# Small products of the last head on four column groups: head 31's last values, its selection, a sum of squares and three sums

## The chip, the cores and the metric

The kernel runs on one NeuronCore of one Trainium2 chip. Its time is the device time of one execution in microseconds; lower is better. TensorE (PE) multiplies, VectorE (DVE), ScalarE (ACT) and GpSimd (POOL) work on vectors, and SyncE (SP) issues nearly all DMAs.

## The reference

One decode step of a transformer block for 4 batches with one token each, all in fp32: an adaptive layer norm, attention with 32 query heads on 8 key and value heads over 4096 cached positions, a gated residual, a second adaptive layer norm, and a token-mixing MLP with F = 1792.

```python
mod = (silu(c) @ w_mod).reshape(4, 6, 1, 512)
sa, ca, ga, sb, cb, gb = (mod[:, k] for k in range(6))
h = layernorm(x) * (1 + ca) + sa
q = (h @ wq) heads;  p = softmax(q k^T / sqrt(128));  o = p v      # k, v: (4, 8, 4096, 128)
x = x + ga * (o @ wo)
h = layernorm(x) * (1 + cb) + sb
u = gelu(layernorm(h)[.., None] * w1 + b1)                          # (4, 512, 1792)
x = x + gb * (u @ w2 + b2)
```

Keys and values are 4 x 8 x 4096 x 128 x 4 bytes each, 134 MB together; they are read once.

## The kernel before, in words

The 32 pairs of batch and key head are called heads 0 to 31 here. SP loads their keys and values in order into a ring of three slots. For each head PE makes the scores, DVE their maximum, ACT the exponentials, DVE turns them (`turn`), PE multiplies them by the values (`values`, `values_narrow`), DVE copies the result out of PSUM (`copy_v`), PE picks and turns the four query rows out of it with the matrix `eight` (`pick`), DVE scales them (`copy_o`), and PE multiplies by the output weights (`project`).

From head 23 on the order of all steps is written out by hand in the string `PLAN`, where `v31.1` is a part of head 31's value products, `V31` the copy, `z31` the turned values, `a31` pick, `A31` copy_o, `I` the addition of the residual `ep`, `p31` project. Each engine runs its own instructions in that order; a wait holds up all that is behind it on that engine.

Head 31's values come as the last data of the cache, in five pieces (blocks of 128 positions 0 to 15, 16 to 23, 24 to 27, 28 to 29, 30 to 31). `values_narrow` multiplies block j with 32 columns of weights (the probabilities) and 128 columns of data (the values), on column group j mod 4 of the array. Blocks 30 and 31 go another way (`values_turned`): the values are the weights, all 128 columns of them, and the four probabilities the moving data, added straight into the PSUM tile `pt` that `pick` then adds the selection to.

Behind `p31` (PSUM tile `pgx`) lies a chain that everything after it needs: DVE makes `a` from `pgx` (`centre`, L617), ACT squares (L622), DVE makes two products (L626, L627), PE spreads `a` to all partitions (`spread_last`, tile `ph`, in two halves), sums the squares over partitions (`deviation`, tile `psq`, L636) and sums three columns (`moments`, tile `pmo`, L641), ACT takes a root (`sd`), DVE forms `vr` (L642, L646, L648) and `hb` (L656), POOL a power (L100), DVE `br` (L658), and then ACT and DVE apply the gelu to 14 pieces of the last batch (L551, L556, L428) while PE contracts them (`py3`, L433).

An fp32 product is two passes on PE: order counts products, the trace counts a weight load (PEld) and a matmul (PE) for each pass. PSUM tiles come from pools: `ps_m` has two slots for tiles tagged `m`, `ps_v` has one slot, tagged `pv`; a tile that takes over a slot waits for the earlier tile's users.

Of the kernel before, what the change touches and what calls it, by code (L numbers as in the profile page):

```python
# [8 lines left out]
F32 = mybir.dt.float32  # L9
# [6 lines left out]
REP = HQ // HKV  # L16
NF = F // 128
EPS = 1e-5
P = 128
NS = B * HKV  # L20
# [8 lines left out]
def adaln_decode(ctx: ExitStack, tc: tile.TileContext, small, x, wmod, wq, kk, kv, vv, wo, out):  # L29
# [8 lines left out]
    ps_v = ctx.enter_context(tc.tile_pool(name="ps_v", bufs=1, space=PSUM))  # L38
    ps_m = ctx.enter_context(tc.tile_pool(name="ps_m", bufs=2, space=PSUM))
    ps_e = ctx.enter_context(tc.tile_pool(name="ps_e", bufs=1, space=PSUM))  # L40
    ctx.enter_context(tc.manual_schedule())
    mm = nc.tensor.matmul
# [41 lines left out]
    mine = g32[:, 8 * (B - 1):8 * (B - 1) + 1]  # L84
    mid = cst.tile([P, 1], F32, name="mid")
    nc.gpsimd.tensor_scalar(mid, mine, 1.0 / D, None, op0=OP.mult)
    eight = g32.rearrange("p (r x) -> p r x", x=8)[:, :, 0]
# [69 lines left out]
    KT, VT, WM = {}, {}, {}  # L157

    def slots():
        return ring.tile([P, 2, SK], F32, name="kv", tag="kv")  # L160
# [35 lines left out]
    def load_key(t, i):  # L196
        nc.sync.dma_start(t, kv[i - 2][:, 0])
        key(t, i)

    def load_v(t, i, cuts):  # L200
        value(t, i)
        src = (kv[i][:, 1] if i < NS - 2 else vv[i - NS + 2]).rearrange("p (j d) -> p j d", d=DH)
        for lo, hi in zip(cuts, cuts[1:]):
            nc.sync.dma_start(VT[i][:, lo:hi], src[:, lo:hi])
# [58 lines left out]
    def turn(i, halves=None):  # L263

        S.pop(i, None)
        if halves is None:
            dv.transpose(PL[i][0], PL[i][0])  # L267
            return
        for n in halves:
            p = PL[i][0][:, n * 512:(n + 1) * 512]  # L270
            dv.transpose(p, p)
# [22 lines left out]
    def values_narrow(i, ks, pv=None):  # L294
        if ks[0] == 0:
            PV[i] = ps_v.tile([P, DH], F32, name="pvn", tag="pv") if pv is None else pv
        pv = PV[i]
        pT = PL[i][0].rearrange("p (k r) -> p k r", r=32)
        top = 32 if i < NS - 1 else 30
        for k in ks:  # L300
            for j in range(4 * k, min(4 * k + 4, top)):
                c = j % 4
                mm(pv[32 * c:32 * c + 32, :], pT[:, j, :], VT[i][:, j, :], start=(k == 0), stop=(j + 4 >= top))  # L303

    def values_turned(i):
        pT = PL[i][0].rearrange("p (k r) -> p k r", r=32)
        OT[i] = pt = ps_m.tile([P, REP], F32, name="pt", tag="m")
        for j in (30, 31):
            mm(pt, VT[i][:, j, :], pT[:, j, 0:32:8], start=(j == 30), stop=False)

    def copy_v(i):
        pv = PV[i]
# [3 lines left out]
    ACC, OT = {}, {}  # L316

    def pick(i):
        po = PV.pop(i)
        n, m = po.shape[-1] // DH, WIDE.get(i, 1)  # L320
        if i in OT:
            mm(OT[i], po, eight, start=False, stop=True)
            return
        pt = ps_m.tile([P, m, REP], F32, name="pt", tag="m")
        OT[i] = pt[:, 0]
        for c in range(n):
            sel = sel4[:, c, :] if n > 1 else eight
            mm(pt, po[:, c * DH:(c + 1) * DH], sel.unsqueeze(1).to_broadcast([P, m, REP]),  # L328
               start=(c == 0), stop=(c == n - 1))
# [7 lines left out]
    def project(i, pa=None, between=None):  # L337
        b, h = divmod(i, HKV)
        oT = OT[i]
        if pa is None:  # L340
            pa = ps_m.tile([P, D], F32, name="pa", tag="m")
            for g in range(REP):
                mm(pa[32 * g:32 * g + 32, :], oT[:, g:g + 1].to_broadcast([P, 32]), wo_t[h][:, g, :],  # L343
                   start=True, stop=True)
        else:
            for g in range(REP):
                for c in range(4):
                    mm(pa[32 * c:32 * c + 32, :], oT[:, g:g + 1].to_broadcast([P, 32]),  # L348
                       wo_t[h][:, g, c * P:(c + 1) * P], start=(g == 0 and h == HKV - 2),
                       stop=(g == REP - 1 and h == HKV - 1))  # L350
                if between and g == 1:
                    between()
        PA[i] = pa
# [242 lines left out]
    mom = cst.tile([P, 3], F32, name="mom")  # L596
    sq = cst.tile([P, 1], F32, name="sq")
# [35 lines left out]

    def deviation():
        ps = ps_m.tile([P, 1], F32, name="psq", tag="m")
        mm(ps, mine.to_broadcast([P, P]), sq, start=True, stop=True)  # L636
        nc.scalar.activation(sd, ps, AF.Sqrt, bias=epsc, scale=1.0 / D)

    def moments():
        pg = ps_m.tile([P, 3], F32, name="pmo", tag="m")  # L640
        mm(pg, mid.to_broadcast([P, P]), mom, start=True, stop=True)  # L641
        dv.tensor_scalar(vr[:, 0:1], pg[:, 0:1], pg[:, 0:1], pg[:, 1:2], op0=OP.mult, op1=OP.subtract)  # L642
        return pg

# [35 lines left out]
    for i in range(NS - HKV):  # L680
# [30 lines left out]
        if i == 2:  # L711
            for t in range(2, 5):
                pm = mod(t)
                dst = prep[:, {2: 1, 3: 2, 4: 3}[t]]
# [12 lines left out]
    pve = pgx = pc = ep = spare = slot = None  # L727
    gates = list(range(2 * REP))
    cuts = {NS - 1: (0, 16, 24, 28, 30, 32), NS - 2: (0, 16, 32)}
    last, halves = [(0, 1, 2, 3), (4, 5), (6,), (7,)], [(0, 1), (2, 3), (4, 5), (6, 7)]  # L730
    PLAN = """
    a23 v24.0 A23 p23 t25.0 P23 F R v24.1 LP25 G s26 t25.1 M H V24 LP26 Q a24 S26 v25.0 N s27 x A24 f p24 g
    x LP27 m26 S27 P24 m27 X26 X27 b26 B26 e26 x b27 v25.1 c g t26.1 l25 t26.0 B27 s28 V25 c g L25
# [1 line left out]
    LK30 t27.1 S29 P26 v27.0 m29 l27 g LK31 T t28.1 X29 LT t28.0 s30 L27 S30 b29 v27.1 B29 e29 l28 m30 V27  # L735
    LV28 L28 a27 g X30 t29.1 t29.0 l29 L29 s31 A27 LV29 b30 p27 x B30 S31 c c m31 e30 P27 X31 v28.0 f LT LV30
    b31 v28.1 B31 f e31 LV31 l30 V28 L30 t30.1 l31 L31 a28 t31.1 A28 p28 v29.0 v29.1 t30.0 f P28 V29 v30.0 a29
    v30.1 A29 LW p29 f v30.2 v30.3 t31.0 P29 g V30 Y y a30 A30 p30 E x v31.0 f v31.1 v31.2 v31.3 V31 z31 a31 I A31 j zy p31
    g T2 za zs zr zc0 zp0 zq zg zp1 zm zc1 T3 zn zw0
    """  # L740
    TABLE = {"s": scores, "S": row_max, "m": turn_max, "X": col_max, "b": spread_max, "B": copy_max, "e": expo,
# [4 lines left out]
    for step in PLAN.split():  # L746
        op, k = step.rstrip("0123456789."), step.lstrip("abcdefghijklmnopqrstuvwxyzABCDEFGHIJKLMNOPQRSTUVWXYZ")
        i, q = (int(n) for n in (k + ".0").split(".")[:2]) if k else (0, 0)
        if op in TABLE:
            TABLE[op](i)  # L750
        elif op in MIX:
            MIX[op]()
        elif op == "t":
            turn(i, [q])
        elif op == "v":
            if i < NS - 2:
                (values if i < NARROW else values_narrow)(i, range(4 * q, 4 * q + 4))
                continue
            if i == NS - 2 and q == 0:
                pve = ps_s.tile([P, 8, P], F32, name="pve", tag="s")  # L760
            values_narrow(i, (last if i == NS - 1 else halves)[q], pve[:, 4 * (NS - 1 - i)])
        elif step == "z31":
            values_turned(i)
        elif op == "p":
            project(i, pgx[:, 4] if i >= NS - 2 else None, mean_last if i == NS - 1 else None)
        elif op == "LT":
            slot = slots()
        elif op == "LK":
            load_key(slot[:, i % 2], i)
        elif op == "LV":  # L770
            load_v(slot[:, i % 2], i, cuts.get(i, (0, 32)))
        elif op == "LW":
            spare = load_wm5()
        elif op == "x":
            mix.expand(spare if mix.n == 6 else None)
        elif op == "f":
            fold_gate(gate, gates[:1])
            del gates[:1]
        elif step == "T":
            nc.scalar.activation(tab, neg1, AF.Exp)  # L780
        elif op == "Y":
            pgx = ps_s.tile([P, 8, P], F32, name="pgx", tag="s")
        elif op == "y":
            pc = fold_groups(ps_m, ACC.pop(B - 1), "m")
        elif op == "E":
            ep = cst.tile([P, P], F32, name="ep")
            dv.tensor_mul(ep, pc, prep[:, 1])
            dv.tensor_tensor_reduce(ep, ep, prep[:, 0], g32[:, 8 * (B - 1):8 * (B - 1) + 1], 0.0, OP.add, OP.add,
                                    tally[:, 0:1])
        elif op == "I":  # L790
            mm(pgx[:, 4], ident, ep, start=False, stop=False)
        elif step == "T2":
            nc.scalar.activation(tab, ones[0:1, 0:1], AF.Sqrt)
        elif step == "T3":
            nc.scalar.activation(tab, neg1, AF.Gelu_apprx_tanh)
        elif op == "za":
            al = centre(pgx[:, 4])
        elif op == "zs":
            squares(pgx[:, 4])
        elif op == "zr":  # L800
            products(al)
        elif op == "zp":
            if i == 0:
                ph = ps_s.tile([P, D], F32, name="ph3", tag="s")
            spread_last(ph, al, range(2 * i, 2 * i + 2))
        elif op == "zc":
            mix.fold_rest(i)
        elif op == "zg":
            pg = moments()
        elif op == "zm":  # L810
            variance(pg)
        elif op == "zn":
            hb, wr, br = affine_last(ph)
        elif op == "j":
            tally_up()
        elif op == "zw":
            modmm(pgx[:, 0], 5, (0,))
# [36 lines left out]
```

## Time and profile before

| what | value |
|---|---|
| time, median of 3 runs | 385.89 us (385.88 to 386.0) |
| the profiled execution, time and span | 385.9 us, 384.1 us |
| PE, PEld busy | 290.1 us (2412 matmuls), 117.2 us (2412 loads) |
| DVE, ACT, POOL busy | 199.4, 111.9, 9.0 us |
| HBM read | 157.32 MB, 410 GB/s over the span |
| granted TensorE clock | mean 0.916; full from about 241 us to the end |

The span is the time from the first to the last instruction of the profiled execution; 1.8 us of its own time lie around it. In rows of the timeline the first number is the start in us from the span's start, the second the time from the first start to the last end of the group, and `x` a count; `128*32` is rows and columns of the array that the instruction uses, and what follows a bracket's arrow is what ended the idle time before the group. In rows of the chain of waits the second number is the time that the chain spends there.

### The profile page before, as it was taken

How to read it: one execution, taken by the hardware profiler on the slowest of the kernel's cores; microseconds unless marked ns; L12 is line 12 of the kernel's file. 1: busy time of each engine (PE TensorE's matmuls, PEld its weight loads, DVE VectorE, ACT ScalarE, POOL GpSimd, SP SyncE). 2: the span in 40 equal slices, each digit the busy share in tenths (PEclk: the TensorE clock that was granted, in tenths of full speed). 3: DMA queues.
4: the chain of work that ended last, by engine and by line, in shares of the span. 5: the costliest groups of instructions: out<-in, count | busy, mean ns of one | idle time of the engine just before them, and what ended most of it. 6: DMA issues, size and time to landing. Idle time of an engine off the chain costs nothing.

```text
span 384.1 us, 5670 instructions
## 1 busy us (share of the span) xinstructions
PE 290.1 (76%) x2412; PEld 117.2 (31%) x2412; DVE 199.4 (52%) x414; ACT 111.9 (29%) x143; POOL 9.0 (2%) x34
## 2 busy tenths in 40 slices
PE   0958484973855928798777879988887887889984
PEld 0112121320222302234222223342222344333673
DVE  0130531440442714556666544657665567778777
ACT  1001210121110111113457310214675104757266
POOL 2100000000000000000000000000000000000000
PEclk9979956697896979989999995999999999999999
DMA  8999999999999999999999999999999999999930
GB/s 332 437 437 437 403 459 427 411 440 433 421 439 437 435 437 433 432 433 432 427 428 433 433 427 432 433 435 437 437 428 430 432 432 431 416 431 426 417 142 4
DMA packets 7410, 157.70 MB, mean 411 GB/s; under 512 B 964, under 2 KB 1236, under 8 KB 1496
## 3 DMA queue, kind: packets, MB, share of 16 engines
q1 hardware_dynamic: 7376, 157.33, 95.5%
q8 instruction: 19, 0.31, 0.3%
q14 instruction: 7, 0.06, 0.0%
q10 hardware_dynamic: 8, 0.00, 0.0%
HBM read 157.32 MB, written 0.01 MB: 410 GB/s over the span
## 4 chain that ended last, share of the span: by engine, by line
DMA 60%; PE 29%; DVE 8%; ACT 2%; issue 1%; POOL 0%; SPq 0%; DVEq 0%; ACTq 0%
DMA kv<-in_kv 58%; PE s L231 7%; PE pv L291 7%; PE s L122 3%; PE qs L138 2%; DVE p L267 2%; DVE m L236 2%; DMA sm<-in_small 2%; PE pa L343 2%; PE pt L328 2%; ACT wo L556 1%; PE pb L251 1%; PE pve L303 1%; PE pm L240 1%; PE pgx L348 1%
## 5 line engine op out<-in xcount | busy, mean ns | idle before, releaser
L231 PE MATMUL s<-kv,QT 128*32 128x512 f32 x512 | 71.8, 685 | 48.7 <-DMA kv<-in_kv 48.4
L236 DVE TENSOR_REDUCE m<-s 128x1 f32<-128x1024 f32 x32 | 39.2, 1224 | 100.7 <-PE s L231 100.7
L261 ACT ACTIVATE p<-s,nm 128x1024 f32<-128x1024 f32 x32 | 35.6, 1114 | 181.2 <-DVE nm L256 181.1
L291 PE MATMUL pv<-kv,p 128*32 128x512 f32 x464 | 67.8, 652 | 0.6 <-DMA kv<-in_kv 0.6
L231 PEld LDWEIGHTS s<-kv,QT 128*32 128x32 f32 x512 | 15.3, 119 | 91.0 <-DMA kv<-in_kv 62.9
L328 PEld LDWEIGHTS pt<-g,po 128*128 128x128 f32 x236 | 30.6, 202 | 27.6 <-issue 20.3
L343 PE MATMUL pa<-wo,oT 128*32 128x512 f32 x240 | 33.7, 633 | 4.9 <-DVE oT L335 4.7
L328 PE MATMUL pt<-g,po 128*128 128x4 f32 (+2 forms) x236 | 33.4, 265 | 1.5 <-DVE po L314 1.0
L267 DVE STREAM_TRANSPOSE p<-p 128x1024 f32<-128x1024 f32 x25 | 30.9, 1235 | 0.0
L314 DVE COPY po<-pv 128x512 f32<-128x512 f32 x29 | 20.0, 689 | 15.7 <-PE pv L291 15.6
L245 DVE TENSOR_REDUCE mx<-pm 1x128 f32<-1x512 f32 x32 | 21.3, 669 | 0.9 <-PE pm L240 0.9
L428 DVE TENSOR_SCALAR u<-hb,wr,sm 128x512 f32<-128x512 f32 x40 | 19.9, 540 | 1.9 <-POOL wr L423 1.0
L485 ACT ACTIVATE u<-u 128x1024 f32<-128x1024 f32 x20 | 20.4, 1052 | 1.5 <-DVE u L428 1.4
L261 ACT ACT_TABLE_LOAD x11 | 14.1, 1283 | 21.9 <-DVE nm L256 21.8
L361 DVE TENSOR_TENSOR acc<-acc,pa 128x512 f32<-128x512 f32 x26 | 17.8, 686 | 2.2 <-PE pa L343 2.1
L251 PEld LDWEIGHTS pb<-neg,mx 1*128 1x128 f32 x64 | 10.0, 194 | 27.6 <-DVE mx L245 25.9
L122 PE MATMUL s<-wm,sT 128*4 128x512 f32 x16 | 9.9, 788 | 10.4 <-POOL sT L108 10.4
L485 ACT ACT_TABLE_LOAD x13 | 16.7, 1283 | 0.2
L291 PEld LDWEIGHTS pv<-kv,p 128*32 128x32 f32 x464 | 13.6, 146 | 6.8 <-issue 2.8
L240 PE MATMUL pm<-ident,m 128*1 128x128 f32 x32 | 8.9, 280 | 7.6 <-DVE m L236 3.5
L251 PE MATMUL pb<-neg,mx 1*128 1x1 f32 x64 | 12.7, 265 | 2.1 <-DVE mx L245 2.1
L240 PEld LDWEIGHTS pm<-ident,m 128*1 128x1 f32 x32 | 2.5, 80 | 34.6 <-DVE rl L280 25.6
(173 smaller groups left out, 227.6 us busy)
## 6 DMA issues: line engine op xcount, KB each, us to landing
kv<-in_kv SPq DMA_DIRECT2D x28, 4096.0 KB, 22.0
wq<-in_wq SPq DMA_DIRECT2D x2, 4096.0 KB, 16.1
wo<-in_wo SPq DMA_DIRECT2D x4, 2048.0 KB
kv<-in_kv SPq DMA_DIRECT2D x4, 2048.0 KB, 21.1
wm<-in_wmod SPq DMA_DIRECT2D x2, 2048.0 KB, 16.1
kv<-in_kk SPq DMA_DIRECT2D x1, 4096.0 KB
kv<-in_vv SPq DMA_DIRECT2D x3, 1024.0 KB
wm<-in_wmod SPq DMA_DIRECT2D x1, 1024.0 KB
```

Of the source, the lines that this page charges most:

```text
L122: mm(s0[0:B, t * D:(t + 1) * D], sT[:, k, :], wm01[:, t, k, :], start=(k == 0), stop=(k == 3))
L231: mm(s[32 * c:32 * c + 32, n * 512:(n + 1) * 512], QT[:, b, h, :], KT[i][:, (n * 4 + c) * 512:(n * 4 + c + 1) * 512], start=True, stop=True)
L236: dv.tensor_reduce(M[i], S[i], axis=AX.X, op=OP.max)
L245: dv.tensor_reduce(mx, M[i].rearrange("o (c r) -> o r c", c=4).unsqueeze(1).to_broadcast([1, 4, 32, 4]), axis=AX.X, op=OP.max)
L251: mm(pb, M[i].rearrange("o c r -> o (c r)"), neg1, start=True, stop=True)
L261: nc.scalar.activation(p, S[i], AF.Exp, bias=M.pop(i), accum_out=l)
L267: dv.transpose(PL[i][0], PL[i][0])
L291: mm(PV[i][32 * q:32 * q + 32, :], pT[:, 128 * k:128 * k + 128:4], VT[i][:, 4 * k:4 * k + 4, :].rearrange("p j d -> p (j d)"), start=(k < ...
L314: dv.tensor_copy(PV[i], pv)
L328: mm(pt, po[:, c * DH:(c + 1) * DH], sel.unsqueeze(1).to_broadcast([P, m, REP]), start=(c == 0), stop=(c == n - 1))
L343: mm(pa[32 * g:32 * g + 32, :], oT[:, g:g + 1].to_broadcast([P, 32]), wo_t[h][:, g, :], start=True, stop=True)
L485: nc.scalar.activation(u, u, AF.Gelu_apprx_tanh)
```

## The change

Four things become four products each, of 32 weight columns, one on each column group of the array, by a new helper `quarters`: the turned values, the selection of head 31, the sum of squares and the three sums. Of head 31's values, blocks 24 to 29 go from `values_narrow` to the turned form too, so `v31` ends with block 23, the copy `V31` stands behind that, and the selection stands between blocks 24 to 27 and blocks 28 to 31. `pmo` moves from the pool `ps_m` to the slot of the value products, `ps_v`, which `py3` takes over later.

```diff
-        top = 32 if i < NS - 1 else 30
+        top = 32 if i < NS - 1 else 24
...
-    def values_turned(i):
+    def quarters(dst, lhs, rhs, start, stop):
+        for c in range(4):
+            mm(dst[32 * c:32 * c + 32], lhs[:, 32 * c:32 * c + 32], rhs, start=start, stop=stop)
+
+    def values_turned(i, js):
         pT = PL[i][0].rearrange("p (k r) -> p k r", r=32)
-        OT[i] = pt = ps_m.tile([P, REP], F32, name="pt", tag="m")
-        for j in (30, 31):
-            mm(pt, VT[i][:, j, :], pT[:, j, 0:32:8], start=(j == 30), stop=False)
+        if js[0] == 24:
+            OT[i] = ps_m.tile([P, REP], F32, name="pt", tag="m")
+        for j in js:
+            quarters(OT[i], VT[i][:, j, :], pT[:, j, 0:32:8], j == 24, j == 31)
...
-            mm(OT[i], po, eight, start=False, stop=True)
+            quarters(OT[i], po, eight, False, False)
...
-        mm(ps, mine.to_broadcast([P, P]), sq, start=True, stop=True)
+        quarters(ps, mine.to_broadcast([P, P]), sq, True, True)
...
-        pg = ps_m.tile([P, 3], F32, name="pmo", tag="m")
-        mm(pg, mid.to_broadcast([P, P]), mom, start=True, stop=True)
+        pg = ps_v.tile([P, 3], F32, name="pmo", tag="pv")
+        quarters(pg, mid.to_broadcast([P, P]), mom, True, True)
...
-    ... v31.0 f v31.1 v31.2 v31.3 V31 z31 a31 I A31 j zy p31
+    ... v31.0 f v31.1 V31 z31.0 a31 z31.1 z31.2 I A31 j zy p31
...
+            values_turned(i, {0: range(24, 28), 1: (28, 29), 2: (30, 31)}[q])
```

PE's order from head 31's values to its projection, before (`pve` the value products, `p` the turned probabilities, `po` the copied value products, `g_122` the matrix that `eight` is a view of, `both` the scaled rows of heads 30 and 31):

```order
L303 MATMUL pve<-kv,p 32x128 [waits DMAHW0_49]
L303 MATMUL pve<-kv,p 32x128 x3
L303 MATMUL pve<-kv,p 32x128 [waits DMAHW1_49]
L303 MATMUL pve<-kv,p 32x128
L309 MATMUL pt<-p,kv 128x4 [waits DMAHW2_49,PE_49]
L309 MATMUL pt<-p,kv 128x4
L322 MATMUL pt<-g_122,po 128x4 [waits DVE_49]
L791 MATMUL pgx<-ep,ident 128x128
L348 MATMUL pgx<-wo_128,both 32x128 [waits DVE_49]
```

The same place after:

```order
L307 MATMUL pt<-p,kv 32x4 [waits DMAHW0_49,PE_49]
L307 MATMUL pt<-p,kv 32x4 x15
L307 MATMUL pt<-g_122,po 32x4 [waits DVE_49]
L307 MATMUL pt<-g_122,po 32x4 x3
L307 MATMUL pt<-p,kv 32x4 [waits DMAHW1_49]
L307 MATMUL pt<-p,kv 32x4 x7
L307 MATMUL pt<-p,kv 32x4 [waits DMAHW2_49]
L307 MATMUL pt<-p,kv 32x4 x7
L796 MATMUL pgx<-ep,ident 128x128
L353 MATMUL pgx<-wo_128,both 32x128 [waits DVE_49]
```

Behind the last piece (DMAHW2) stood two products of full width and the selection; now there stand eight of a quarter's width, and the selection is ahead of it. The residual's product (`ep`) keeps full width and its place.

PE's order around the two sums, before:

```order
L632 MATMUL ph_2418<-a,ident 128x128 [waits DVE_49]
L632 MATMUL ph_2418<-a,ident 128x128
L636 MATMUL psq<-sq,g_122 128x1 [waits Activation_49]
L641 MATMUL pmo<-mom,mid 128x3 [waits DVE_49,PE_49]
L632 MATMUL ph_2418<-a,ident 128x128 x2
L516 MATMUL pc<-u,sm 32x128 x4
```

And after:

```order
L637 MATMUL ph_2445<-a,ident 128x128 [waits DVE_49]
L637 MATMUL ph_2445<-a,ident 128x128
L307 MATMUL psq<-sq,g_122 32x1 [waits Activation_49]
L307 MATMUL psq<-sq,g_122 32x1 x3
L307 MATMUL pmo<-mom,mid 32x3 [waits DVE_49]
L307 MATMUL pmo<-mom,mid 32x3 x3
L637 MATMUL ph_2445<-a,ident 128x128 x2
L521 MATMUL pc<-u,sm 32x128 x4
```

The places are the same; the sums are of a quarter's width between full-width products, and `pmo` no longer waits for PE's own earlier work. The order of the instructions on DVE, ACT, POOL and SP is unchanged.

More of the change, by code (lines that the diff above doesn't have):

```diff
@@ L729, in adaln_decode @@
     cuts = {NS - 1: (0, 16, 24, 28, 30, 32), NS - 2: (0, 16, 32)}
-    last, halves = [(0, 1, 2, 3), (4, 5), (6,), (7,)], [(0, 1), (2, 3), (4, 5), (6, 7)]
+    last, halves = [(0, 1, 2, 3), (4, 5)], [(0, 1), (2, 3), (4, 5), (6, 7)]
     PLAN = """
@@ L737, in adaln_decode @@
     b31 v28.1 B31 f e31 LV31 l30 V28 L30 t30.1 l31 L31 a28 t31.1 A28 p28 v29.0 v29.1 t30.0 f P28 V29 v30.0 a29
-    v30.1 A29 LW p29 f v30.2 v30.3 t31.0 P29 g V30 Y y a30 A30 p30 E x v31.0 f v31.1 v31.2 v31.3 V31 z31 a31 I A31 j zy p31
+    v30.1 A29 LW p29 f v30.2 v30.3 t31.0 P29 g V30 Y y a30 A30 p30 E x v31.0 f v31.1 V31 z31.0 a31 z31.1 z31.2 I A31 j zy p31
     g T2 za zs zr zc0 zp0 zq zg zp1 zm zc1 T3 zn zw0
@@ L761, in adaln_decode @@
             values_narrow(i, (last if i == NS - 1 else halves)[q], pve[:, 4 * (NS - 1 - i)])
-        elif step == "z31":
-            values_turned(i)
+        elif op == "z":
+            values_turned(i, {0: range(24, 28), 1: (28, 29), 2: (30, 31)}[q])
         elif op == "p":
```

## The prediction

> **What bounds the kernel now.** I read the page's chain by engine first, then the chain of waits from 365 us on, then the timeline of PE, DVE and ACT at the four places that the change touches.
>
> ```profile
> span 384.1 us, 5670 instructions
> DMA 60%; PE 29%; DVE 8%; ACT 2%; issue 1%; POOL 0%; SPq 0%; DVEq 0%; ACTq 0%
> ```
>
> Until about 365 us the loads of the cache set the pace, and nothing there changes. Behind it the chain runs:
>
> ```profile
> 365.75 1.89 PE pve L303 x60
> 367.71 0.58 PE pt L309 x4
> 368.29 0.22 PE pt L322 x2
> 368.51 0.33 PE pgx L791 x2
> ...
> 369.98 0.37 DVE a L617 x2
> 370.39 0.71 PE ph L632 x4
> 371.11 0.16 PE psq L636 x2
> 371.27 0.26 PE pmo L641 x2
> ...
> 372.23 0.66 DVE hb L656
> 372.89 0.29 DVE br L658
> ...
> 373.27 1.52 ACT wo L551 x2
> ```
>
> All four changed products are on it; from L551 on the rest hangs on ACT and moves as one. So the gain is how much sooner L551 starts.
>
> **What a narrow product costs.** Full width, then a quarter's width with one column of data (the mean's sum, L668), and what follows that:
>
> ```profile
> 367.71 0.58 PE L309 MATMUL pt<-p,kv 128*128 128x4 f32 x4
> L309 PE MATMUL pt<-p,kv 128*128 128x4 f32 x4 | 0.6, 250 | 0.1
> 369.23 0.22 PE L668 MATMUL pmu<-part,tally 128*32 128x1 f32 x8
> L668 PE MATMUL pmu<-part,tally x8: 167/168/170, 369.2 to 369.3; 128*32 128x1 f32 x8
> 369.29 0.62 PE L348 MATMUL pgx<-wo,both 128*32 128x128 f32 x16
> ```
>
> Four full passes of 0.25 take 0.58: they start (0.58 - 0.25)/3 = 0.11 apart. Eight narrow ones of 0.17 take 0.22: seven steps in 0.05, 0.007 each, so a round over the four groups takes 0.03, and the next line starts 0.06 behind the first, two rounds later. A product thus falls from 0.22 to 0.06, and its end comes 0.08 sooner. With 128 columns of data a round takes (0.62 - 0.27)/3 = 0.12. The new products have one, three or four columns, nearest to L668: I take 0.03 and keep 0.11 as the other end.
>
> **What a change of width costs.**
>
> ```profile
> 371.37 0.69 PE L632 MATMUL ph<-a,ident 128*128 128x128 f32 x4
> 371.99 0.16 PEld L516 LDWEIGHTS pc<-u,sm 128*32 128x32 f32 x8
> 369.12 0.24 PEld L668 LDWEIGHTS pmu<-part,tally 128*32 128x32 f32 x8
> 368.77 0.64 PE L348 MATMUL pgx<-wo,both 128*32 128x128 f32 x16
> ```
>
> L516 waits for no other engine there, yet its first load comes at 371.99, 0.07 before the last full-width matmul ends (372.06). At equal width L668's loads start at 369.12, 0.29 before L348's end. So at each change of width the loads wait until 0.07 before the end. The new order moves one such change (from the turned values to L791) and adds two (into `psq` and out of `pmo`).
>
> **Part 1, the last values.** Before:
>
> ```profile
> 366.75 0.09 DVE L586 DVE_READ_ACCUMULATOR2_ANT rowsum<- 128x1 f32 x1
> 366.88 0.16 PEld L303 LDWEIGHTS pve<-kv,p 128*32 128x32 f32 x8
> 367.21 0.14 PEld L303 LDWEIGHTS pve<-kv,p 128*32 128x32 f32 x4 [0.17 <-DMA kv<-in_vv]
> 367.67 0.29 DVE L314 COPY po<-pve 128x128 f32<-128x128 f32 x1 [0.83 <-PE pve L303]
> 367.68 0.52 PEld L309 LDWEIGHTS pt<-p,kv 128*128 128x128 f32 x4 [0.33 <-PE pve L303]
> 368.15 0.36 PE L322 MATMUL pt<-g,po 128*128 128x4 f32 x2
> 368.34 0.30 PEld L791 LDWEIGHTS pgx<-ep,ident 128*128 128x128 f32 x2
> 368.37 0.47 PE L791 MATMUL pgx<-ep,ident 128*128 128x128 f32 x2
> 368.55 0.16 DVE L335 TENSOR_TENSOR both<-pt,rl 128x4 f32<-128x4 f32 x1 [0.59 <-PE pt L322]
> 368.77 0.38 PEld L348 LDWEIGHTS pgx<-wo,both 128*32 128x32 f32 x16
> ```
>
> The piece with 28 and 29 is in at 367.2; the last one, of the same size, lands between that and 367.64, since L309 loads at 367.68. From there: six full passes, end of L322 at 368.51, L335 at 368.55, projection at 368.77.
>
> After: block 23's last round starts about 366.79, 0.09 ahead of the next piece's load, and ends at 367.06. DVE is free from 366.84 on, so the copy runs 367.11 to 367.40, and the selection loads at 367.45 (0.05 for each step between engines, as from L335's end at 368.71 to 368.77). Blocks 24 to 27 (8 rounds, 0.24) start about 366.95 and are covered by this copy; without it, at 0.11 a round, they would hold the selection until 367.83. Selection 0.06 and blocks 28, 29 0.12 end at 367.63; so the last blocks start then, wherever up to 367.6 their piece lands. Their four rounds, 0.03 from load to matmul (as 367.68 to 367.71 for L309) and the last one's 0.17, of which a round is counted already, end at 367.93 instead of 368.51. L335 then ends at 368.13.
>
> The projection gains less. L791 is of full width and now stands between narrow products: loads at 367.93 - 0.07 = 367.86, ends 0.49 later (its 368.34 to 368.84 before) at 368.35, and the projection loads at 368.28, though L335 would let it at 368.18. So 368.28 for 368.77: **-0.49**. Up to L617 all hangs on this projection; ACT's table load and DVE's copy beside it have ended or move along.
>
> **Part 2, the two sums.** Before:
>
> ```profile
> 370.39 0.71 PE L632 MATMUL ph<-a,ident 128*128 128x128 f32 x4
> 370.88 0.30 PEld L636 LDWEIGHTS psq<-sq,g 128*128 128x128 f32 x2
> 370.94 0.33 PE L636 MATMUL psq<-sq,g 128*128 128x1 f32 x2
> 371.15 0.35 PE L641 MATMUL pmo<-mom,mid 128*128 128x3 f32 x2
> 371.30 0.26 ACT L637 ACTIVATE sd<-psq,epsc 128x1 f32<-128x1 f32 x1 [0.47 <-PE psq L636]
> 371.55 0.29 DVE L642 TENSOR_SCALAR vr<-pmo 128x1 f32<-128x1 f32 x1 [0.54 <-PE pmo L641]
> 371.75 0.20 DVE L646 SCALAR_TENSOR_TENSOR vr<-smv,sd,pmo 128x1 f32<-128x1 f32 x1
> 372.88 0.20 ACT L795 ACTIVATE tab<-neg 1x1 f32<-1x1 f32 x1
> ```
>
> In these times (0.49 comes off all): `ph` ends at 371.10, so `psq`, now narrow, loads at 371.03 instead of 370.88 and ends at 371.03 + 0.03 + 0.03 + 0.02 + 0.17 = 371.28 (load to matmul, one round, the last group's place in it, the matmul) instead of 371.27. It gains nothing. `pmo` follows without a change of width and ends 0.06 later, at 371.34 instead of 371.50: -0.16. L642 moves to 371.39, but L646 also needs `sd`, ready at 371.31 + 0.26 + 0.05 = 371.62, so it moves by 0.13. The second half of `ph` loads at 371.27 and ends 0.08 sooner, in time for `hb`. POOL, `br` and L551 follow L646: **-0.13**. ACT's table load ends its small activation at 373.09, 0.05 before the new L551 at 373.14; beyond that 0.05 more gain would be lost to it.
>
> **What costs nothing.** `pmo`'s old wait for PE's own work is over long before. In the shared slot `py3` gets such a wait; it is queued with the wait for L551, more than 2 us behind `pmo`'s readers, so ACT hides it. PE issues 66 more passes (88 for 22). No DMA and no queue of SP or POOL is passed.
>
> **Sum.** -0.49 - 0.13 = -0.62. The profiled execution's own 385.9 equals the median 385.89, so 385.3 us, 0.16% less. About 0.2% (0.77 us) is what a measurement of this kernel can tell from no change.
>
> **The rivals.** First, code. The page says
>
> ```profile
> q8 instruction: 19, 0.31, 0.3%
> PE 290.1 (76%) x2412; PEld 117.2 (31%) x2412; DVE 199.4 (52%) x414; ACT 111.9 (29%) x143; POOL 9.0 (2%) x34
> 369.64 0.22 PEld L512 LDWEIGHTS pc<-yw,g 128*32 128x32 f32 x8
> ```
>
> so a fetch brings 16 KB, 4824/19 = about 254 PE instructions. The DMA view has one fetch in the window from 369.3 to 370.3 and the next in that from 372.6 to 372.8, when the DMA engines idle and nothing delays it:
>
> ```profile
> q8 instruction: 1, 0.02, 5.8%
> q8 instruction: 1, 0.02, 36.5%
> ```
>
> A fetch of 0.9 us (5.8% of 16 engines' 1.0 us) in the first window ends at about 370.3. Between L512 and 372.7 PE runs some 110 instructions (twice the matmuls of L512 to L209 in the timeline), and 108 of the added ones stand ahead of L512 (144 for 36): the boundary that asked for the second fetch moves up to L512, to about 369.2. If PE holds only one block ahead, the block needed there is not in before 370.3, `ph` starts at about 370.95 instead of 369.90, and the time is 385.28 + 1.05 = 386.3: slower than before. It decides once the block lands over 0.6 us behind L512. For it: the fetch is asked for ahead of the added instructions and gets no sooner. Against: no wait of PE here is put to code. [...]
>
> Second, the rounds do not shrink: 0.11 each. Then blocks 24 to 27 end at 367.83, ten more rounds at 368.9, L335 moves by +0.5 and, with L791, the projection by +0.6, the sums by +0.1: 386.6. It decides from 0.07 a round. L668's row is against it. [...]
>
> Third, the added changes of width cost less than L516's: then -0.58 from L335 and -0.20, 385.1.
>
> **How the numbers follow.** My forecast, 385.1 to 385.5: 0.60. Cheap changes of width, 384.9 to 385.1: 0.15. Code, about 386.3: 0.17. Rounds, 386.6: 0.08. Under 385.12 lie the third rival and 0.08 of the forecast's edge: faster 0.23. Over 386.66 lie the upper edges of the other two: slower 0.05. The rest, 0.72, is within 0.2%. The range 384.9 to 386.4 leaves out the rounds and the edge of the code case.
>
> **What the profile will show.** L307's 40 products ahead of L796 in rounds of 0.03; the copy at 367.1; L335 near 367.97, and L353's first load set by L796, near 368.28; L617 near 369.49; `psq` loading 0.07 before `ph` ends and `sd` no earlier against `a`; L642 0.16 and L551 0.13 earlier against `a`. A gap of PE without a releaser between L517 and L637 is the code case. I am wrong if those rounds are longer, or if L353 follows L335.

## The result and the profile after

The changed kernel takes 388.75 us (median of 6 runs, 388.16 to 389.73), the kernel before beside it 385.91 (6 runs, 385.76 to 386.04): a ratio of 1.0076, 95% interval 1.0061 to 1.009. It is slower by 2.8 us where 385.3 was forecast. Some runs of most kernels here lie 1 to 4 us above the others of the same kernel; the ratios take them in, the medians hardly move with them.

The profiled execution of the changed kernel has a time of 388.16, the lowest of its six. From its page: the span, the chain by engine, the busy times, and the queue that brings instructions.

```profile
span 386.4 us, 5802 instructions
PE 295.6 (77%) x2478; PEld 118.7 (31%) x2478; DVE 199.7 (52%) x414; ACT 111.9 (29%) x143; POOL 9.0 (2%) x34
q8 instruction: 19, 0.31, 0.3%
DMA 48%; PE 36%; DVE 9%; ACT 4%; issue 1%; POOL 0%; SPq 0%; ACTq 0%
```

The averages hardly tell the two kernels apart. The timeline of PE's weight loads does (start, length of the group, idle time ahead of it and what ended that):

```profile
367.03 1.33 PEld L303 LDWEIGHTS pve<-kv,p 128*32 128x32 f32 x48
368.34 0.47 PEld L307 LDWEIGHTS pt<-p,kv 128*32 128x32 f32 x32
369.04 0.16 PEld L307 LDWEIGHTS pt<-g,po 128*32 128x32 f32 x8 [0.23 <-DVE po L319]
369.10 0.37 PEld L307 LDWEIGHTS pt<-p,kv 128*32 128x32 f32 x32
369.49 0.30 PEld L796 LDWEIGHTS pgx<-ep,ident 128*128 128x128 f32 x2
369.91 0.38 PEld L353 LDWEIGHTS pgx<-wo,both 128*32 128x32 f32 x16
370.26 0.24 PEld L673 LDWEIGHTS pmu<-part,tally 128*32 128x32 f32 x8
370.40 0.16 PEld L353 LDWEIGHTS pgx<-wo,both 128*32 128x32 f32 x7
371.80 0.25 PEld L353 LDWEIGHTS pgx<-wo,both 128*32 128x32 f32 x9 [1.24 <-issue]
371.94 0.33 PEld L517 LDWEIGHTS pc<-yw,g 128*32 128x32 f32 x8
372.76 0.52 PEld L637 LDWEIGHTS ph<-a,ident 128*128 128x128 f32 x4 [0.29 <-DVE a L622]
```

The reader is to see the ninth row. In the middle of the projection's second half, between two products that need nothing new, PE stands still for 1.24 us, and no releaser is named. Behind the gap the chain runs as before:

```profile
372.35 0.35 DVE L622 SCALAR_TENSOR_TENSOR a<-pgx,mu,prep 128x128 f32<-128x128 f32 x1 [1.51 <-PE pgx L353]
373.72 0.26 ACT L642 ACTIVATE sd<-psq,epsc 128x1 f32<-128x1 f32 x1 [0.51 <-PE pmo L307]
373.81 0.29 DVE L647 TENSOR_SCALAR vr<-pmo 128x1 f32<-128x1 f32 x1 [0.43 <-PE pmo L307]
375.54 0.81 ACT L556 ACTIVATE wo<-hb,br,wr 128x512 f32<-128x512 f32 x1
```

Against the rows of before, point by point. One of them is shown nowhere above:

```profile
365.46 1.58 PEld L303 LDWEIGHTS pve<-kv,p 128*32 128x32 f32 x56
```

| point | before | after | later by |
|---|---|---|---|
| first load of `v31` (L303) | 365.46 | 367.03 | 1.57 |
| projection, first load | 368.77 | 369.91 | 1.14 |
| `a` (L617, now L622) | 369.98 | 372.35 | 2.37 |
| first gelu (L551, now L556) | 373.27 | 375.54 | 2.27 |

The first line is not the change's: six other kernels with the change or a part of it start `v31` at 365.35 to 365.55. In the windows view (busy time and count of PE, PEld, DVE, ACT, POOL, then the granted clock, the DMA share, GB/s) the clock of TensorE was half in this execution from 310 to 320 us, in before's it was full; row of before, then of after.

```profile
309.90:320.40 10.50, 9.02 (x88) 4.58 (x82) 7.29 (x19) 2.33 (x3) 1.31 (x3) 1.00 1.00 427
```

```profile
309.90:320.40 10.50, 9.71 (x51) 3.02 (x43) 4.89 (x13) 0.00 (x0) 0.55 (x1) 0.51 0.97 417
```

Whether the late start comes of this stretch is open: no run tests it. Three other kernels start `v31` as late, at 366.9 to 367.2, one of them without the change (64 idle instructions, below); the sums alone (368.04) and the 168 idle instructions (366.65) start late too.

From `v31` to the projection the change gains 0.43, the gap then loses about 1.2, and from `a` to the first gelu it gains 0.10. The experiments below show that the 1.57 is not the cause: PE goes on at about 371.7 whether `v31` started at 365.4 or at 367.0.

### The profile page after: what moved, and what is told of

It is laid out like the page before. It is cut to its first block, busy times and chain, and to the rows that moved or that the text cites. A ratio compares the mean times of both kernels' runs of the same rounds, so it can differ in the third digit from the quotient of the medians.

```text
span 386.4 us, 5802 instructions
## 1 busy us (share of the span) xinstructions
PE 295.6 (77%) x2478; PEld 118.7 (31%) x2478; DVE 199.7 (52%) x414; ACT 111.9 (29%) x143; POOL 9.0 (2%) x34
## 4 chain that ended last, share of the span: by engine, by line
DMA 48%; PE 36%; DVE 9%; ACT 4%; issue 1%; POOL 0%; SPq 0%; ACTq 0%
DMA kv<-in_kv 35%; PE s L231 11%; PE pv L291 8%; DMA wm<-in_wmod 6%; DMA kv<-in_kk 5%; DVE m L236 3%; PE pa L348 3%; DVE p L267 2%; PE pt L333 2%; PE s L122 2%; DMA sm<-in_small 2%; PE pb L251 1%; ACT wo L561 1%; PE py L444 1%; PE pm L240 1%
## 5 line engine op out<-in xcount | busy, mean ns | idle before, releaser
L231 PE MATMUL s<-kv,QT 128*32 128x512 f32 x512 | 77.5, 727 | 44.7 <-DMA kv<-in_kv 41.9
L348 PE MATMUL pa<-wo,oT 128*32 128x512 f32 x240 | 35.4, 664 | 4.8 <-DVE oT L340 4.6
L122 PE MATMUL s<-wm,sT 128*4 128x512 f32 x16 | 8.3, 680 | 10.5 <-POOL sT L108 10.5
```

What stands on the lines that cost most here:

```text
L231: mm(s[32 * c:32 * c + 32, n * 512:(n + 1) * 512], QT[:, b, h, :], KT[i][:, (n * 4 + c) * 512:(n * 4 + c + 1) * 512], start=True, stop=True)
```

## Experiments

All were compared with the kernel before on the same chip. The queue `q8` brings the program in packets of 16 KB (0.31 MB in 19), by the forecast's sum, an estimate, some 254 instructions of PE each; what one packet brings is called a block here. Two theories stood: the new instructions move the first use of a block to a time at which its packet has not come yet, and the gap is the wait for it (code); or the new products, their order and their slot are slow by themselves (width). A third, that the half clock from 310 to 320 us is the loss (clock), stands in the first expectations.

**The change with 168 idle PE instructions (42 products) spread over heads 9 to 20.**

```diff
     def sums(i):
...
+        if i in range(9, 19):
+            for c in range(4):
+                mm(pl[32 * c:32 * c + 32], PL[i][1].to_broadcast([P, 32]), eight, start=True, stop=True)
+        if i in (19, 20):
+            mm(pl, PL[i][1].to_broadcast([P, P]), eight, start=True, stop=True)
```

> The changed kernel, with 42 idle products (168 PE instructions) added at heads 9 to 20, where PE waits for loads anyway: they only write the sum of exponentials again. [...] The added instructions move the boundaries by 168, to the middle of blocks 24 to 27 (about 367.2 us) and into L521 behind the second half of ph, so no gap of more than 0.5 us stands between the selection and L637, and the time falls to 385.3 to 386.0. Rival theory width: the gap comes from the switch between narrow and full products or from the number of narrow products itself; then the gap stays in L353 and the time stays at 388.2 to 389.7. Rival theory clock: most of the loss is TensorE's clock at half speed at 310 to 320 us; then the gap may move but the time stays above 387.

Measured 388.76 us (4 runs; ratio 1.0076, 1.0053 to 1.0098). PE's loads in the timeline:

```profile
364.13 0.43 PEld L308 LDWEIGHTS pve<-kv,p 128*32 128x32 f32 x16 [0.72 <-issue]
...
367.96 0.35 PEld L312 LDWEIGHTS pt<-p,kv 128*32 128x32 f32 x21
370.04 0.17 PEld L312 LDWEIGHTS pt<-p,kv 128*32 128x32 f32 x10 [1.72 <-issue]
371.49 0.63 PEld L358 LDWEIGHTS pgx<-wo,both 128*32 128x32 f32 x16
```

The gap has left the projection and stands behind the 21st load of `z31.0`. That is where counting puts it: 84 loads ahead of the old place are 7 of the projection's second half, 8, 16, 2, 32 and 8 of the groups before it, and 11 of the 32 of `z31.0`. So the place follows the count of instructions and not the work. The forecast that it would cost nothing there was a miss: this block was wanted at about 368.3 and its packet came at 367.83 to 368.76. The first row is a gap of the same kind one block earlier (its packet came at 361.91 to 362.86): from there to the second gap PE issues 16, 8, 2, 32, 48 and 21 loads, 127 and as many matmuls, 254 instructions.

**The kernel before with 64 idle PE instructions (heads 9 to 12) and nothing of the change.**

> The kernel before, with 16 idle products (64 PE instructions) added at heads 9 to 12, and none of the change. Theory code: the boundary that PE crossed at about 372.4 us moves 64 instructions up, into L516 ahead of ph (about 369.9), and the block for it is asked for at about 365.3 instead of 366.2; from the two fetches seen under load it is in 3.5 to 5.5 us after the request, at 368.8 to 370.8, so a gap of 0 to 0.9 us appears in L516 and the time is 385.9 to 386.8. Rival width: no product is of another width, so 385.9. Rival clock: 385.9 with a granted clock like before, unless half clock comes by chance.

Measured 386.82 us (6 runs; ratio 1.0022, 1.0008 to 1.0036): 0.97 us slower with 64 instructions that nobody waits for. Its profiled execution had `v31` at 367.04, so PE came late to the place; the folds' eight loads, 0.24 long in before, took 0.43:

```profile
371.17 0.43 PEld L519 LDWEIGHTS pc<-u,sm 128*32 128x32 f32 x8
```

That is a wait of about 0.2 us; no trace shows an execution that comes there on time.

**The change without the two sums, and the two sums alone.** First `psq` and `pmo` in their old form:

```diff
-        quarters(ps, mine.to_broadcast([P, P]), sq, True, True)
+        mm(ps, mine.to_broadcast([P, P]), sq, start=True, stop=True)
...
-        pg = ps_v.tile([P, 3], F32, name="pmo", tag="pv")
-        quarters(pg, mid.to_broadcast([P, P]), mom, True, True)
+        pg = ps_m.tile([P, 3], F32, name="pmo", tag="m")
+        mm(pg, mid.to_broadcast([P, P]), mom, start=True, stop=True)
```

> The change without its two sums: L636 and L641 stay one product of full width each, pmo stays in the pool of two slots. 108 PE instructions are added, all ahead of the projection's second half. Theory code: the gap of about 1.2 us (or more, where PE comes there sooner) stays in L353, time 388.0 to 389.8. Rival width: the gap stays if it comes with the values, and goes if it came with the sums (then 385.4). Rival clock: 388 to 389 with half clock at other times in each run.

Then the values and the selection in their old form, with quartered sums:

> The kernel before, with only the two sums in four products each and pmo in the value products' slot. 24 PE instructions are added, behind the last boundary but one. Theory code: the boundary moves from the last matmuls of L521 to its middle, behind ph's second half, so no gap on the path; the sums give -0.1 us, time 385.7 to 385.9. Rival width: the two added changes of width cost more than they give, 385.9 to 386.2. Rival clock: a spread of runs of more than 0.5 us above 386, as the changed kernel has.

Without the sums 389.75 us (4 runs; ratio 1.0101, 1.0082 to 1.0121); the sums alone 385.75 (11 runs; ratio 1.0002, 0.9993 to 1.0012). The first has the gap at the same load, 2.61 long because PE is on time here:

```profile
368.92 0.16 PEld L353 LDWEIGHTS pgx<-wo,both 128*32 128x32 f32 x7
371.69 0.40 PEld L353 LDWEIGHTS pgx<-wo,both 128*32 128x32 f32 x9 [2.61 <-issue]
369.10:371.60 2.50, 0.24 (x8) 0.00 (x0) 0.23 (x2) 0.00 (x0) 0.00 (x0) 0.79 0.04 13
371.70:380.70 9.00, 8.92 (x113) 7.07 (x117) 5.94 (x20) 5.62 (x9) 0.76 (x2) 0.50 0.01 3
```

The last row is a second cost: for nine microseconds behind the gap the granted clock is half, which the profiled execution of the whole change was spared. `v31` is on time here, and the loss is no smaller, so the third theory is out. The sums alone put 12 more loads ahead of the place where PE needs the block; on before's times it is reached at 372.0 or later, behind 371.7, so no gap is due. Its profiled execution has none, but it is the slowest of the eleven (388.12) and starts `v31` only at 368.04, so it says nothing of one on time.

**Why the block is late: the last load cut to a quarter.** `WM[5]`, 1 MB, is the last load of the program and lands at 370.0 in before. This kernel leaves three quarters of it out and uses the first quarter four times.

```diff
-        nc.sync.dma_start(t[:, 0:4], wmod[2][:, 1])
-        WM[5] = t[:, 0:4]
+        nc.sync.dma_start(t[:, 0:1], wmod[2][:, 1, 0:1])
+        WM[5] = t[:, 0:1].to_broadcast([P, 4, D])
```

> The change as it is, but the last load of the program (WM[5], 1 MB, which lands at 370.0 behind the cache) brings only its first quarter, and the products that read it use that quarter four times; the rest of the matrix is left out. Theory 'code waits for loads': the block of instructions that TensorE lacks is asked for at about 367 us and its packet only starts at 369.4 because the load's packets stand ahead of it on the same DMA engines. With 0.25 MB the loads end at about 368.1, the packet starts between 367.5 and 368.1, TensorE goes on 2.3 us after that start, at 369.8 to 370.4, so the gap in L353 shrinks from 1.24 (or 2.6 when TensorE is on time) by 1.3 us or more, and the time falls to 386.0 to 387.3 us. Rival 'the wait is a fixed latency of the fetch': packet and gap stay (TensorE goes on at about 371.7), time 388.3 to 389.2. Rival 'TensorE's half clock': the time stays near 388.7 with no gap to explain it.

Measured 386.32 us (12 runs; ratio 1.0022, 1.0005 to 1.0039), and the gap in the profiled execution, with `v31` at 366.91, is 0.70:

```profile
370.28 0.16 PEld L353 LDWEIGHTS pgx<-wo,both 128*32 128x32 f32 x7
371.14 0.25 PEld L353 LDWEIGHTS pgx<-wo,both 128*32 128x32 f32 x9 [0.70 <-issue]
```

The packet came at 368.39 for 369.42. Of the loss, 2.4 of 2.8 us went with 0.75 MB of data that has nothing to do with instructions. PE went on later than expected (371.1 for 369.8 to 370.4): the packet started late, 368.39 for 367.5 to 368.1, since `v31` was late, and took 1.38 us.

**Issuing that load later, nothing left out.** A memset of one column by DVE makes the DMA wait for a step of `PLAN`:

```diff
-        nc.sync.dma_start(t[:, 0:4], wmod[2][:, 1])
...
+    def load_late():
+        dv.memset(WM[5][:, 0, 0:1], 0.0)
+        nc.sync.dma_start(WM[5], wmod[2][:, 1])
...
-    ... p30 E x v31.0 f v31.1 V31 ...
+    ... p30 E LZ x v31.0 f v31.1 V31 ...
```

> [...] Theory 'code waits for loads': the packet of instructions finds the DMA engines free between 367.5 and about 368.9 and runs at 367.5 to 368.5; TensorE goes on at about 369.9; where it reaches the place at 369.07 (as in values alone) the gap is 0.8 instead of 2.6, and the time is 386.0 to 387.0 us. [...] Rival 'fixed latency': no change of the gap, 388.3 to 389.2. Rival 'the late load is late': L209's products wait for it behind 372.3 and hold up what follows, 387 or more, with a DMA wait in that line.

Measured 389.86 us (5 runs; ratio 1.0115, 1.0097 to 1.0134): a miss. SP's row and PE's:

```profile
365.31 0.33 SPq L197 DMA_DIRECT2D kv<-in_wmod  x1
371.80 0.40 PEld L356 LDWEIGHTS pgx<-wo,both 128*32 128x32 f32 x9 [2.88 <-issue]
```

Step E ended at 365.1 and not at 366.8 as in the change's profile, so the load was issued at 365.3; its data closed up with the cache's and ended at 370.03, and the packet came at 369.45 as ever. The edit did not do what it was for; the rival 'fixed latency', which forecast 388.3 to 389.2 and the same gap, is not answered by it. No run shows the 368.9 that the forecast takes for the start of this load's data: in the three kernels below whose late load starts apart from the cache's data, they start 0.9 to 1.0 us behind the issue (367.08 and 368.0, 367.85 and 368.75, 367.42 and 368.39).

**Fewer instructions, and both together.** The quartered form only for blocks 28 to 31, 24 loads fewer ahead of the folds; then this with the late load of the experiment above.

```diff
-        top = 32 if i < NS - 1 else 24
+        top = 32 if i < NS - 1 else 28
...
-    ... v31.1 V31 z31.0 a31 z31.1 z31.2 I ...
+    ... v31.1 v31.2 V31 z31.0 a31 z31.1 I ...
...
```

> The change with fewer instructions, nothing left out: the turned and quartered products only for blocks 28 to 31 instead of 24 to 31, so 48 instructions of TensorE fewer before the folds; blocks 24 to 27 are narrow value products again, and DVE's copy follows them. Theory 'code': the boundary of the block (recorded instruction 4546) now stands 48 later in the program, at the end of L521's folds; TensorE goes on there at about 371.7 as before, but less work is left behind it: ph's loads come at 371.8 instead of 372.8 us, so the time is about 387.5 to 388.0, with a gap of 1.2 to 1.8 us between L521 and L637. Rival 'the new products themselves are slow (order of accumulation, slots, width changes)': the gain over before stays away in proportion, no gap in L521 or behind it, and the time is anything between 385.9 and 388.7.

> Both edits: quarters only for blocks 28 to 31, and the last 1 MB load issued later; nothing left out. Theory 'code waits for loads': the packet runs at 367.5 to 368.5, TensorE may go on from 369.9, and it reaches the boundary, now at the end of L521, at about 369.9 to 370.0: gap 0 to 0.2 us. Then the change shows its own gain, 0.5 us of the path: 385.2 to 385.7 us, faster than before. Rival 'fixed latency': 387.5 to 388.0 as without the late load. Rival 'the late load is late' : L209 waits behind 372 us, 386 or more.

Fewer instructions: 387.30 us (5 runs; ratio 1.0036, 1.0024 to 1.0048); with the late load: 388.57 (6 runs; ratio 1.0067, 1.0053 to 1.0082). The first is just under its forecast, the second a miss by 3 us. Rows of the first:

```profile
369.49 0.23 PEld L521 LDWEIGHTS pc<-u,sm 128*32 128x32 f32 x7
371.64 0.10 PEld L521 LDWEIGHTS pc<-u,sm 128*32 128x32 f32 x1 [1.92 <-issue]
```

and of the second, with SP's:

```profile
367.08 0.33 SPq L197 DMA_DIRECT2D kv<-in_wmod  x1
373.70 0.10 PEld L524 LDWEIGHTS pc<-u,sm 128*32 128x32 f32 x1 [2.29 <-issue]
```

The gap moved by 24 loads exactly, to the eighth load of the folds, and its end stayed near 371.7. The second had `v31` at 367.15 and the load issued at 367.08; the data ran until 371.92, the packet came at 371.22, and PE went on at 373.70. In these two runs the later load only took the packet with it or left it where it was.

**The load behind the packet.** The memset moved behind DVE's copy `V31`: with fewer instructions, with the whole change, and in the kernel before as a control.

```diff
-    ... p30 E LZ x v31.0 f v31.1 v31.2 V31 z31.0 ...
+    ... p30 E x v31.0 f v31.1 v31.2 V31 LZ z31.0 ...
```

> Quarters only for blocks 28 to 31, nothing left out, and the last 1 MB load (WM[5]) issued behind DVE's copy of V31 (367.4 where TensorE is on time), two microseconds behind the place that the late load had, where it was in fact issued at 365.3 and still closed up with the cache. Issue to first packet was 1.0 us, so its data run 368.5 to 370.9. Theory 'the packet of code runs only when the data queued ahead of it are through' (in the ten traces so far it starts between 0.4 us before and 0.7 us behind the last data packet, whether that is at 367.7, 369.6 or 371.9): the cache's pieces are through at 367.2, the packet runs 367.3 to 368.4, TensorE may go on from 369.8, and it reaches the boundary at 369.7 (gap 0 to 0.2 us). Time 385.2 to 385.8 us. Rival 'latency of the fetch or of the request, not the data': packet again at 369.4 and gap 1.9, time 387.0 to 387.5. Rival 'the late load is late': its landing at 371.2 (372.8 where TensorE is late) holds L209's products and then L551, 386 or more, with a DMA wait there.

> The change as it is, nothing left out, with the last 1 MB load issued behind DVE's copy of V31. Theory 'the packet runs only when the data ahead are through': TensorE may go on from 369.8 (on time) instead of 371.7, and reaches the boundary in L353 at 369.0: gap 0.8 us or less for 2.6; where TensorE is late by 1.5 us the gap is gone or below 0.4. Time 385.6 to 386.6 us. Rival 'latency, not the data': 388.2 to 389.8 as in the change. Rival 'the late load is late': as in the kernel beside it.

> Control: the kernel before, none of the change, with the last 1 MB load issued behind DVE's copy of V31 (367.7). Theory 'the packet runs only when the data ahead are through': the kernel before has no gap to lose, so nothing is won; 385.7 to 386.1. If the late load alone made it faster by 0.3 us or more, the load and not the code would be what the two kernels beside it win by; if slower by 0.3 or more, L209's products wait for it.

Fewer instructions 385.69 us (11 runs; ratio 0.999, 0.9977 to 1.0002), the whole change 386.21 (12 runs; ratio 1.0012, 1.0 to 1.0024), the control 386.01 (12 runs; ratio 0.9998, 0.999 to 1.0007); before 385.97. The first, SP, PE, and the gelu at the end of the path:

```profile
367.85 0.33 SPq L197 DMA_DIRECT2D kv<-in_wmod  x1
369.39 0.24 PEld L520 LDWEIGHTS pc<-yw,g 128*32 128x32 f32 x8
369.61 0.28 PEld L524 LDWEIGHTS pc<-u,sm 128*32 128x32 f32 x8
370.16 0.52 PEld L640 LDWEIGHTS ph<-a,ident 128*128 128x128 f32 x4 [0.27 <-DVE a L625]
372.93 1.52 ACT L559 ACTIVATE wo<-hb,br,wr 128x512 f32<-128x512 f32 x2
```

No gap: the packet came at 367.05. The whole change keeps a short one, since it needs the block earlier:

```profile
367.83 0.30 PEld L801 LDWEIGHTS pgx<-ep,ident 128*128 128x128 f32 x2
367.96 0.16 DVE L343 TENSOR_TENSOR both<-pt,rl 128x4 f32<-128x4 f32 x1 [0.62 <-PE pt L310]
368.25 0.38 PEld L356 LDWEIGHTS pgx<-wo,both 128*32 128x32 f32 x16
369.65 0.25 PEld L356 LDWEIGHTS pgx<-wo,both 128*32 128x32 f32 x9 [0.76 <-issue]
370.21 0.35 DVE L625 SCALAR_TENSOR_TENSOR a<-pgx,mu,prep 128x128 f32<-128x128 f32 x1 [1.02 <-PE pgx L356]
373.39 0.81 ACT L559 ACTIVATE wo<-hb,br,wr 128x512 f32<-128x512 f32 x1
```

In the control the packet came at 367.38 for before's 369.34, and there is neither gain nor loss, so the late load in itself is worth nothing; it only lets the packet through. This settles the cause: nothing of the products changed, the packet came 2.3 to 2.4 us sooner, the gap went or shrank, and the loss went with it but for 0.2 us in the whole change. A fixed latency of the fetch is out too.

**The same with the memset behind step `f`,** off the path:

> The kernel with quarters for blocks 28 to 31 and the late load once more, nothing left out; only the place of the issue differs: the memset stands behind DVE's step f (366.8 where TensorE is on time) and not behind the copy of V31. There it stood in the path (the selection waited for the memset, 0.06 us on DVE, and the load landed at 372.85, behind which L209's products waited 0.6 us). Theory: the load is issued at 367.0, its first packets come at 368.5 or later, so the block of instructions still runs before them, 367.1 to 368.5, no gap; WM[5] lands at about 372.0; the path is 0.06 to 0.1 us shorter: 385.3 to 385.6 us, faster than before beyond the interval. Rival 'the packet is overtaken again': the load's packets start at 368.0 and the block's packet falls behind them, gap 1.5 us or more at L521, 386.8 to 387.5.

Measured 385.59 us against 385.96 (11 and 15 runs): 8 of the 11 lie at 385.43 to 385.70, three at 387.0 to 387.2, and the ratio, 1.0002 (0.999 to 1.0013), leaves it open. No gap in the profiled execution, `WM[5]` in at 372.06, and L209's products (L212 here) no longer wait for it, as they did for 0.62 us in the first kernel above:

```profile
370.19 0.52 PEld L640 LDWEIGHTS ph<-a,ident 128*128 128x128 f32 x4 [0.32 <-DVE a L625]
372.29 0.24 PEld L212 LDWEIGHTS pgx<-kv,sT 128*32 128x32 f32 x8
```

By medians it is the best of all kernels here, 0.37 us under before; that it beats before is likely and not shown.

**All packets side by side**, from the trace's list of DMA packets (us), for the block that the gap waits for:

| kernel | `v31` starts | data on the queue end | packet | PE goes on |
|---|---|---|---|---|
| the change | 367.03 | 369.60 | 369.42 to 370.37 | 371.80 |
| without the sums | 365.55 | 369.60 | 369.36 to 370.29 | 371.69 |
| fewer instructions | 365.35 | 369.58 | 369.44 to 370.40 | 371.64 |
| late load | 365.39 | 370.03 | 369.45 to 370.39 | 371.80 |
| fewer, late load | 367.15 | 371.92 | 371.22 to 372.10 | 373.70 |
| a quarter of the load | 366.91 | 367.70 | 368.39 to 369.77 | 371.14 |
| the change, load behind `V31` | 365.37 | 367.16 (the load starts at 368.39) | 367.16 to 368.34 | 369.65 |

PE goes on 1.2 to 1.6 us behind the end of the packet in these seven. The load 127 ahead of the gap's (counted below), where PE enters the block before, lies in the middle of `v31`, by estimate about 0.7 us behind its start (26 of 48 loads in 1.33 us). From there to the packet it is 0.8 to 1.1 us in the last two rows, where the data are through when the packet starts, and 1.7 to 3.4 us in the others, where it starts 0.1 to 0.7 us before their end. With the 168 idle instructions PE entered the block before at 364.13, in the midst of the cache's loads, and the packet came 3.7 us later.

The place can be counted outright. In the windows view the second count is PE's loads; from the start to the end of the gap the change has

```profile
0.00:371.75 371.75, 287.01 (x2261) 112.62 (x2261) 189.02 (x383) 102.51 (x131) 8.27 (x32) 0.89 0.99 424
```

and the same view has 2261 loads ahead of the gap's end in the seven other traces with one (the other six rows and the 168 idle instructions), whatever stands there; the earlier gap of the idle instructions has 2134, 127 fewer.

## Why the prediction was wrong

The step that failed is in "What costs nothing": "PE issues 66 more passes (88 for 22)." They cost no time of PE and yet were what the kernel lost by, since 54 of them stand ahead of the gap. The forecast named this as its first rival, gave it 0.17, and weighed against it that "no wait of PE here is put to code". That was no evidence: before has no such wait only because it needs the block later. Counting 30 loads on from the gap of the kernel with fewer instructions (eighth of L516, then 12 of `ph`, `psq`, `pmo`, `ph`, 8 of L516, the tenth of the next 16), before needs it at the tenth load of this row, the one with 2261 ahead of it, at about 372.4:

```profile
372.12 0.46 PEld L516 LDWEIGHTS pc<-kv,sm 128*32 128x32 f32 x16
```

Its packet came at 369.34 to 370.27, so by the 1.2 to 1.6 us of the table it could go on from 371.5 to 371.9, an estimate. It missed the wait by about 0.7 us.

The rival's mechanism held, its size did not: "ends at about 370.3" was right for the packet (370.37), but PE was taken to go on there. It went on at 371.80, and `ph` loaded at 372.76 for the rival's 370.95: 386.3 + 1.8 = 388.1, the profiled execution's 388.16. The median is 0.6 above that, and what it is made of is open. The kernel without sums and the one with the late load, whose executions had the half clock behind their gap (0.50 in the first; in the second the eight loads of `yw` took 0.60 as in the first, for 0.33 in the change), end at 389.9 and 389.8, so that runs of the change above 388.2 had it too is likely; no trace of them was taken. The rival put the gap between L517 and L637; it stands 9 loads ahead of L517.

The rival's condition was "If PE holds only one block ahead". The traces agree with it: no packet of the table starts before PE has entered the block before, 127 loads ahead of the need; the shortest lag is 0.8 us. In before PE did not wait at this count, though the packet came at 369.34 there; in the change it waited 1.24 us.

The rest came out nearly as worked:

- **Narrow rounds, 0.03.** The 32 passes of L307, eight rounds, take 0.43 to 0.46 in all, the last one's 0.17 among it, so a round takes 0.03 to 0.04; `psq` and `pmo` load 0.06 apart. The rival of 0.11 a round is out.
- **Part 1.** With the load behind `V31` and PE on time, `both` comes at 367.96 and the projection's load at 368.25, where 367.97 and 368.28 were predicted. Some of this closeness is luck: `v31` started at 365.37 here for before's 365.46, and from its start to the projection's load it is 2.88 for 3.31 in before, a gain of 0.43 for the predicted 0.49. The change of width at L801 sets the projection, as said: its matmuls end at 368.32, and the projection's first load stands 0.07 ahead of that, though `both` was done at 368.12.
- **Part 2, -0.13.** From `a` to the first gelu 3.18 and 3.19 for 3.29: -0.10 to -0.11.
- **The sum, 385.3.** The whole change with the load behind `V31` had a gap of 0.76 and a time of 386.06 in its profiled execution: without the gap 385.30. This is arithmetic on one execution, with the 0.09 by which its `v31` was early; no run of the whole change without a gap was made.

## What to carry to other kernels

Instructions that cost PE no time had a price here: 54 more loads ahead of the gap, and a wait of 1.24 us. So count PE's instructions to the next block's edge (a block was 254 of them by the counts above), and ask when its packet can come while loads are still running. A kernel without a gap can stand right beside one (before, by about 0.7 us), so compare the edge's place in both programs, and test a suspicion with idle instructions added far ahead: here the gap moved with the count, by 84 loads for 84, and that pointed to code. Ending the loads earlier shrank the gap (to 0.70, with a quarter of the last load); starting the last load behind the packet shrank it to 0.76 in the whole change and took it away with fewer instructions. Making the load merely later left the packet where it was (369.45) or took it along (371.22).

## What the runs showed of the hardware

- PE's code came in packets of 16 KB (0.31 MB in 19), and the waits stood at fixed counts: 2261 loads lay ahead of the gap in eight traces, 2134 ahead of the one before it, so a block held about 127 loads and their matmuls. Taking 24 loads away moved the gap by 24 loads, adding 84 moved it by 84.
- PE went on 1.2 to 1.6 us after the packet's end in the seven traces of the table (the packets were 0.88 to 1.38 us long).
- The packet waited behind data: it started 0.8 to 1.1 us behind the entry into the block before where the data had ended by then, 1.7 to 3.7 us where they had not, and it came 2.3 to 2.4 us sooner when the last load was issued behind `V31`. Which of the 16 engines' queues lines them up, and in what order, no run here tells.
- Behind the gap of 2.61 us (without the sums) the granted clock was 0.50 from 371.7 to 380.7; behind that of 1.24 us, in the change, it was 1.00 from 371.8 to 384.0. Other traces show PE's loads stretched behind the gap, against the same loads of the change or of before: behind 2.88 us (late load) eight took 0.60 for 0.33, from 372.02 on; behind 1.72 us (the 168 idle instructions) sixteen took 0.63 for 0.38, from 371.49 on; behind 1.92 us (fewer instructions) sixteen took 0.84 for 0.46, from 373.61 on. Behind 0.70 us (the short load) they took the same 0.46, from 373.76 on. What the gap has to do with the clock is open.
